# FNet mixing and an ELU layer: w_in folded with two products a chunk after sums and differences of its rows

## The chip, the core and the metric

The kernel runs on one core of one Trainium2 chip. The profile names its engines PE (TensorE, matrix products; PEld is its loading of weights), DVE (VectorE), ACT (ScalarE), POOL (GpSimd) and SP (SyncE, which here only issues DMAs). The metric is the device time of one execution in microseconds (us), the median over several.

## What is computed

```python
X = np.fft.fft(x, axis=1)          # x: (8, 3008, 256) float32
X = np.fft.fft(X, axis=2).real
t = X.reshape(24064, 256)
h = t @ w_in                       # w_in: (256, 2048), float64
g = np.where(h > 0, h, np.exp(np.minimum(h, 0)) - 1)
out = g @ w_out                    # w_out: (2048, 256), float64
```

The real part of the two transforms is cosine times cosine less sine times sine: along the sequence and along the 256 channels. The weights come as 64-bit floats, and the kernel turns them to 32 bits itself.

## The kernel before

**The channel transform is folded into w_in.** x is real, so channels d and 256-d are first added and subtracted (e and o), which leaves 129 cosine channels and 127 sine channels. The matrix of channel cosines and sines, CC, is multiplied into w_in once: Wc = cos @ w_in (128 rows) and Ws = -sin @ w_in (127 rows, and in its last row the 129th cosine channel). h is then Wc times the sequence cosines of e plus Ws times the sequence sines of o, plus the 129th channel, which lies in wex and Rb and is added on VectorE.

**Chunks of weights.** w_in and w_out are cut into eight chunks of 512 KB each. A `Chunk` is loaded (`load`, on SP) into a home `raw` and turned into 32-bit floats in steps: `fields` (L204: two TENSOR_SCALAR on VectorE, L212 and L218, take exponent and mantissa out of the high words), `power` (L224: ScalarE), `round` (L234: GpSimd adds low and high mantissa; for the very first chunk VectorE, L243) and `scale` (L249: L255 on VectorE puts sign and exponent together, then GpSimd multiplies; for the first chunk VectorE, L264). Homes are shared by chunks: those of chunks 0, 1 and 2 of w_in are used again by chunks 5, 6 and 7, and later by other tiles.

**fold_chunk (L371)** multiplies a chunk of w_in (256 rows, 256 columns; its rows lie in two halves of 128 on the partitions) by CC: two results, 128x256 for Ws and 128x256 for Wc, each as two products over 128 rows that add up in one PSUM bank, "H". `put_chunk` (L385) copies the results to Ws and Wc with two ScalarE instructions. `spread_last_row` (L390) sends the last row of Ws through DRAM into columns of wex.

**The main loop** runs over 47 tiles of 256 columns and, in each, over eight *slots*. A slot takes two of the 16 blocks of 128 rows of the hidden layer: `mm_P` (H<-Rr,Wc), `even_part` (E on VectorE, L728), `mm_Q` (H<-Ir,Ws, which adds to the same bank and so must wait until E is read), `h_minus` (L738), two ScalarE passes and two VectorE passes for the ELU (L754), and the products with w_out (pA to pD<-G). From the third tile on the products with w_out use seven products for eight, from sums of G on GpSimd and sums of w_out (`sum_weights`, WT). Tiles 0 and 1 are worked on together in the first sixteen slots and use w_out plainly; the slots of block pair i need chunk i of w_in folded and chunk i of w_out scaled.

**The sequence transform.** For each of the eight batches `fold_x` (L435) folds x: for each of four pieces j, e{j} = lo + hi, o{j} = lo - hi over channels (L441, operations e and o), a copy c{j} of channel 0 (L461), a memset z{j} of a pad column, then sums and differences between pieces (E0, EO0, O0 and so on). For the first batch all this is on VectorE, at the start; for the others on GpSimd, spread over the slots by the list FOLDS. `Dft` multiplies the folds by cosine and sine matrices MC and puts the results into rings Rr and Ir.

**The order of the work.** Each step is entered into a list of events with a due time (`at`, in slots of PERIOD = 4.8), which are made by hand; the events are sorted by due time, and compute instructions are kept in that order on each engine (`pin`). DMAs are placed by the framework. So every engine runs a fixed sequence, and waits at the first instruction whose input isn't there. Before the first product 46 products on zeros run on PE. The bank tag "H" has three buffers; fold_chunk and the slots take them in turn.

Of the kernel before, what the change touches and what calls it, by code (L numbers as in the profile page):

```python
# [9 lines left out]
FP = mybir.dt.float32  # L10
# [5 lines left out]
ALU = mybir.AluOpType  # L16
# [39 lines left out]

def _chan_consts():

    c = np.arange(256)
    d = np.arange(129)  # L60
    cos = np.cos(2.0 * np.pi * ((c[:, None] * d[None, :]) % 256) / 256)
    d = np.arange(1, 128)
    sin = -np.sin(2.0 * np.pi * ((c[:, None] * d[None, :]) % 256) / 256)
    m = np.concatenate([cos[:, :128], sin, cos[:, 128:]], axis=1)
    return np.ascontiguousarray(
        m.reshape(2, 128, 256).transpose(1, 0, 2).reshape(128, 512)
    ).astype(np.float32)


# [9 lines left out]
def kernel(  # L79
# [80 lines left out]
        return L  # L160


    CC = cpool.tile([128, 512], FP, tag="CC")
    w2 = cpool.tile([128, NF * ND], FP, tag="w2")
    Wc = cpool.tile([128, NDFF], FP, tag="Wc")
    Ws = cpool.tile([128, NDFF], FP, tag="Ws")
# [5 lines left out]
    w1 = {}  # L172

    class Chunk:

        def __init__(self, src, dst, raw, tmp, shared):
            self.src, self.dst, self.home, self.tmp_tag = src, dst, raw, tmp
            self.shared = shared  # L180

        def load(self):
            dst = self.dst()
            if not wide:
                nc.sync.dma_start(out=dst, in_=self.src)
                return
            home = self.home
            if isinstance(home, tuple):
                tag, bufs, size = home
                home = spool.tile([128, size], FP, tag=tag, bufs=bufs, name="raw")  # L190
            words = home[:, 0:1024].bitcast(I32)
            self.raw = words.rearrange("p (n w) -> p n w", w=2)
            n = dst.shape[1]
            nc.sync.dma_start(
                out=words.rearrange("p (a b) -> p a b", a=n), in_=self.src.bitcast(I32)
            )
# [37 lines left out]
        def round(self):  # L234
# [11 lines left out]
                )  # L246
            )

        def scale(self):  # L249

            if not wide:
                return
            lo, hi, dst = self.parts()
            pin(
                nc.vector.scalar_tensor_tensor(  # L255
                    out=self.t, in0=hi, scalar=-(2**31), in1=self.t,
                    op0=ALU.bitwise_and, op1=ALU.bitwise_or,
                )
            )
            if self.shared:  # L260
                gtt(dst, dst, self.t.bitcast(FP), ALU.mult)
                return
            pin(
                nc.vector.scalar_tensor_tensor(  # L264
                    out=dst, in0=dst, scalar=2.0**-20,
                    in1=self.t.bitcast(FP), op0=ALU.mult, op1=ALU.mult,
                )
            )

    def w1_dst(c):  # L270
        q, half = divmod(c, 2)
        if q not in w1:
# [24 lines left out]
            IN_HOMES[c],  # L297
            IN_TMP[c],
            c > 0,
        )  # L300
        for c in range(8)
    ]
# [4 lines left out]
            OUT_HOMES[c],  # L307
            OUT_TMP[c],
            True,
        )  # L310
        for c in range(8)
    ]
# [39 lines left out]
    def mm(out_, lhsT, rhs, start, stop=True):  # L352
        pin(
            nc.tensor.matmul(  # L354
                out_, lhsT=lhsT, rhs=rhs, start=start, stop=stop, skip_group_check=True
            )
        )
# [7 lines left out]
    def act(o, i, func=AF.Copy, **kw):  # L365
        pin(nc.scalar.activation(out=o, in_=i, func=func, **kw))  # L366
# [3 lines left out]

    def fold_chunk(c):  # L371

        q, half = divmod(c, 2)
        ps = folds[c] = bank("H")
        for n, part in enumerate((128, 0)):
            for h in range(2):
                mm(
                    ps[:, 256 * n : 256 * n + 256],
                    CC[:, h * 256 + part : h * 256 + part + 128],
                    w1[q][:, h, half * 256 : half * 256 + 256],  # L380
                    n == 0 and h == 0,
                    h == 1,
                )

    def put_chunk(c):  # L385
        cols = slice(c * 256, (c + 1) * 256)
        for n, dst in enumerate((Ws, Wc)):
            act(dst[:, cols], folds[c][:, 256 * n : 256 * n + 256])

    def spread_last_row(q):  # L390
        c = slice(q * 256, (q + 1) * 256)
# [38 lines left out]
        gtt(W[3], W[1], b21, ALU.add)  # L430


    OC = slice(0, 6 * 127)

    def fold_x(L, engine_of, pieces):  # L435

        ops = {}

        def op(key, o, a, b, f):
            tt = lambda o, a, b, f: pin(  # L440
                engine_of(key).tensor_tensor(out=o, in0=a, in1=b, op=f)  # L441
            )
            n = o.shape[1]
            cuts = [n * i // pieces for i in range(pieces + 1)]
            for i in range(pieces):
                c = slice(cuts[i], cuts[i + 1])
                ops[key, i] = lambda c=c: tt(o[:, c], a[:, c], b[:, c], f)

        E, O = [], []
        for j in range(4):  # L450
            e = spool.tile([128, 6 * 128], FP, tag=f"e{j}", bufs=1, name=f"e{j}")
            o = spool.tile([128, 6 * 127 + 1], FP, tag=f"o{j}", bufs=1, name=f"o{j}")
            ev = e.rearrange("p (m d) -> p m d", d=128)
            ov = o[:, OC].rearrange("p (m d) -> p m d", d=127)
            src = L[j].rearrange("p (m d) -> p m d", d=ND)
            if j in (1, 2):
                src = src[:, ::-1]
            lo, hi = src[:, :, 1:128], src[:, :, 255:128:-1]
            op(f"e{j}", ev[:, :, 1:128], lo, hi, ALU.add)
            ops[f"c{j}", 0] = lambda e=ev[:, :, 0:1], s=src[:, :, 0:1]: pin(  # L460
                engine_of("c").tensor_copy(out=e, in_=s)  # L461
            )
            op(f"o{j}", ov, lo, hi, ALU.subtract)
            E.append(e)
            O.append(o)
        ops["x1", 0] = lambda: act(L[1][0:1, 5 * ND :], L[0][0:1, 0:ND])
        for j in (1, 3):
            ops[f"z{j}", 0] = lambda o=O[j]: pin(
                nc.gpsimd.memset(o[:, 6 * 127 :], 0.0)
            )  # L470
        P = [o[:, OC] for o in O]
        op("E0", E[0], E[0], E[1], ALU.add)
        op("E2", E[2], E[2], E[3], ALU.add)
        op("EO0", E[1], E[0], E[2], ALU.add)
        op("EO1", E[3], E[0], E[2], ALU.subtract)
        op("O0", P[0], P[0], P[1], ALU.subtract)
        op("O2", P[2], P[2], P[3], ALU.subtract)
        op("EO2", P[1], P[0], P[2], ALU.subtract)
        op("EO3", P[3], P[0], P[2], ALU.add)
        return [E[1], E[3], O[1], O[3]], ops  # L480

    FOLDS = (
        "c0 e0 c3 e3 c2 e2 x1 c1 e1 E0 E2 EO0 o0 o3 o2 o1 z1 z3 O0 O2 EO2 EO1 EO3".split()
    )

    def fold_first(L):
# [45 lines left out]
    class Dft:  # L532
# [5 lines left out]
            self.ring = ring if ring is not None else (Ir if ri else Rr)  # L538

        def mms(self, par, ps):  # L540
            width = 1 if self.first else 127 if self.ri else 128
            dft_mms(ps, self.ri, self.kodd, par, self.stat, width)
            if par:
                self.pb = ps
            else:
                self.pa = ps
# [515 lines left out]
        state["x_even"] = Dft(0, 0, 0, fold_first(L_first), ring=Rb, first=True)  # L1062

    at(-25.5, load_rest)
    at(-25.0, lambda: fold_now("z1 z3 c3 e3"))
    at(-24.9, w1_chunks[0].scale)
    at(-24.8, lambda: fold_now("o3 c2 e2 E2 o2 O2"))
    at(-24.5, begin_x_even)
    at(-24.4, lambda: fold_now("c0 e0 c1 e1 E0 EO0"))
    at(-20.7, lambda: load_mats(1, 1))  # L1070
    at(-20.6, w1_chunks[5].load)
    at(-20.5, w2_chunks[5].load)
# [25 lines left out]
    for chunk, k in (  # L1098
        (w2_chunks[0], 0),
        (w1_chunks[2], 1),  # L1100
        (w1_chunks[3], 2),
        (w2_chunks[1], 3),
        (w1_chunks[4], 4),
        (w2_chunks[2], 5),
        (w1_chunks[5], 6),
        (w2_chunks[3], 7),
        (w1_chunks[6], 8),
        (w2_chunks[4], 9),
        (w1_chunks[7], 10),
        (w2_chunks[5], 11),  # L1110
        (w2_chunks[6], 12),
        (w2_chunks[7], 14),
    ):
        t = k * T
        first = ((0.96, 0.96, 0.97, 1.9), (3.0, 3.05, 3.06, 4.22), (0.95, 0.96, 0.97, 4.2))
        dt = first[k] if k < 3 else (-0.5, 0.05, 0.06, 2.95)
        for d, fn in zip(dt, (chunk.fields, chunk.power, chunk.round, chunk.scale)):
            at(t + d, fn)
    for chunk, t in (
# [156 lines left out]
    at(27 * T + 1.0, lambda: ext_rows(0, vtt))  # L1276
    at(27 * T + 1.46, lambda: ext_side(3))
    at(28 * T + 1.35, lambda: ext_rows(1, gtt))
    fold_keys = [(k, p) for k in FOLDS for p in range(2 if k[0] not in "czx" else 1)]
    n_big = sum(k[0] not in "czx" for k, _ in fold_keys)  # L1280
    for b in range(1, NB):
        s0 = (b - 1) * steps_b
        l0 = s0 - 8 if b > 1 else 5.2
# [4 lines left out]
        for key in fold_keys:  # L1288
            at(
                int(f0 + n * (f1 - f0) / n_big) * T + 1.3,  # L1290
                lambda key=key: state["ops"][key](),
            )
            n += key[0][0] not in "czx"
        for n, (ri, kodd) in enumerate(((0, 0), (1, 0), (0, 1), (1, 1))):
            at_dft(
                s0 + (28, 34, 38, 42)[n], 2, b, ri, kodd,
# [56 lines left out]
```

## Time and profile before

| | |
|---|---|
| median of 8 runs | 1972.76 us (1971.12 to 1979.74) |
| the profiled execution | 1971.63 us, of which the span of the profile is 1969.8 us |
| busy: PE, DVE, ACT, POOL | 1957.5, 1274.7, 869.5, 1333.0 us |
| fold products H<-w,CC | 64 records, 15.1 us busy |
| scaling and rounding of weights on POOL, 128x512 | 1.3 us each |
| one sum of G on POOL, 128x256 | 728 ns |
| a copy of a fold result on ACT, 128x256 | 378 ns |

How to read it: the span is from the first instruction to the last. A 32-bit product of PE leaves two MATMUL records in the profile, so the 32 fold products are 64 records. A record's own time overlaps the next one's, so what a product takes is read from the distance of two starts. In a row of the timeline the first number is the start in us, the second the duration, and the bracket at the end tells the idle time before it and who ended it. A row "x8" is eight instructions in a row.

### The profile page before, as it was taken

What the parts mean: (1) busy time and instruction counts of PE and PEld (TensorE: products, weight loads), DVE (VectorE), ACT (ScalarE), POOL (GpSimd) and SP (SyncE); (2) the same over time, 40 slices, a digit from 0 to 9 for tenths busy, and PEclk for the clock granted to TensorE, in tenths of its full rate; (3) what the DMA queues carried; (4) which work ended last, traced back from release to release, by engine and by line L of the source; (5) the groups of instructions that cost most, each with busy time, mean ns of one, the idle gap of its engine ahead of it and who ended that gap; (6) DMA issues with size and microseconds to landing.
All of it is one profiled execution on the core that took longest, in us unless ns stands there. A gap on an engine that the chain in (4) does not pass through costs nothing.

```text
span 1969.8 us, 26831 instructions
## 1 busy us (share of the span) xinstructions
PE 1957.5 (99%) x8900; PEld 1662.8 (84%) x8900; DVE 1274.7 (65%) x2325; ACT 869.5 (44%) x1667; POOL 1333.0 (68%) x1804
## 2 busy tenths in 40 slices
PE   9999999999999999999999999999999999999998
PEld 5888888888888888888888888888888888888887
DVE  8866656765666656666566665676566665666666
ACT  4654444444444444444344444444434444344443
POOL 3588657775677766777567875778657776455655
PEclk9999999999999999999999999999999999999999
DMA  9056200121001110021100301013010110100101
GB/s 367 22 21 91 38 11 20 47 48 22 12 20 46 45 27 11 18 65 27 26 18 13 79 12 26 11 19 91 6 20 12 20 22 15 16 12 12 22 10 24
DMA packets 255610, 71.08 MB, mean 36 GB/s; under 512 B 243998, under 2 KB 244786, under 8 KB 255088
## 3 DMA queue, kind: packets, MB, share of 16 engines
q1 hardware_dynamic: 250896, 56.52, 15.0%
q0 software_dynamic: 2400, 12.59, 1.9%
q8 instruction: 70, 1.15, 0.2%
q14 instruction: 68, 0.56, 0.1%
q10 hardware_dynamic: 2176, 0.26, 0.1%
HBM read 44.50 MB, written 24.80 MB: 35 GB/s over the span
## 4 chain that ended last, share of the span: by engine, by line
PE 95%; DVE 2%; issue 1%; POOL 1%; ACT 0%; DMA 0%; DVEq 0%; POOLq 0%
PE H L354 39%; PE pD L354 16%; PE pB L354 16%; PE pC L354 16%; PE pA L354 8%; DVE E L728 0%; DMA wex<-wx 0%; POOL xl L145 0%; POOL G L363 0%; DVE v L360 0%; DVE G L754 0%; ACT G L366 0%; ACT M L366 0%; DVE Ir L360 0%; DVE u L360 0%
## 5 line engine op out<-in xcount | busy, mean ns | idle before, releaser
L363 POOL TENSOR_TENSOR G<-G 128x256 f32<-128x256 f32 x1440 | 1034.8, 728 | 566.9 <-DVE G L754 455.3
L728 DVE SCALAR_TENSOR_TENSOR E<-Rb,wex,H 128x256 f32<-128x256 f32 x752 | 328.1, 478 | 613.5 <-PE H L354 609.7
L366 ACT ACTIVATE G<-H 128x512 f32<-128x512 f32 x376 | 224.5, 597 | 953.2 <-DVE G L738 953.1
L354 PE MATMUL H<-Ir,Ws 128*128 128x256 f32 x1504 | 387.2, 380 | 1.9 <-DVE E L728 1.8
L354 PE MATMUL H<-Rr,Wc 128*128 128x256 f32 x1504 | 386.4, 379 | 0.0
L354 PE MATMUL pC<-G,WT 128*128 128x256 f32 x1440 | 369.5, 379 | 0.0
L354 PEld LDWEIGHTS H<-Rr,Wc 128*128 128x128 f32 x1504 | 285.1, 190 | 54.1 <-issue 2.5
L354 PEld LDWEIGHTS H<-Ir,Ws 128*128 128x128 f32 x1504 | 277.0, 189 | 51.6 <-DVE E L728 5.3
L354 PEld LDWEIGHTS pC<-G,WT 128*128 128x128 f32 x1440 | 273.6, 190 | 37.2
L738 DVE SCALAR_TENSOR_TENSOR G<-E,H 128x512 f32<-128x512 f32 x376 | 257.3, 684 | 37.1 <-PE H L354 1.6
L754 DVE SCALAR_TENSOR_TENSOR G<-G,H 128x512 f32<-128x512 f32 x376 | 255.9, 680 | 25.9 <-ACT G L366 25.9
L754 DVE SCALAR_TENSOR_TENSOR G<-M,G 128x512 f32<-128x512 f32 x376 | 257.0, 684 | 0.0
L366 ACT ACTIVATE G<-G 128x512 f32<-128x512 f32 x376 | 233.2, 620 | 0.0
L354 PE MATMUL pA<-G,w 128*128 128x256 f32 x784 | 229.4, 379 | 0.2 <-POOL w L363 0.2
L354 PE MATMUL pB<-G,w 128*128 128x256 f32 x784 | 229.2, 379 | 0.0
L354 PE MATMUL pD<-G,w 128*128 128x256 f32 x784 | 229.2, 379 | 0.0
L366 ACT ACTIVATE M<-G 128x512 f32<-128x512 f32 x376 | 224.3, 596 | 0.0
L366 ACT ACTIVATE M<-M 128x512 f32<-128x512 f32 x376 | 220.9, 588 | 0.1
L354 PE MATMUL pD<-G,WT 128*128 128x256 f32 x720 | 214.4, 379 | 1.6 <-DVE v L360 1.6
L354 PE MATMUL pB<-G,WT 128*128 128x256 f32 x720 | 214.4, 379 | 0.5 <-POOL G L363 0.5
L354 PEld LDWEIGHTS pA<-G,w 128*128 128x128 f32 x784 | 148.9, 190 | 20.8 <-POOL w L363 0.6
L354 PEld LDWEIGHTS pD<-G,w 128*128 128x128 f32 x784 | 149.0, 190 | 20.2
(132 smaller groups left out, 1385.4 us busy)
## 6 DMA issues: line engine op xcount, KB each, us to landing
out_dram<-ot SPq DMA_DIRECT2D x496, 32.0 KB
xl<-in_x_dram SPq DMA_DIRECT2D x16, 768.0 KB
out_dram<-ot SPq DMA_DIRECT2D x256, 2.0 KB
Rb<-r SPq DMA_DIRECT2D x10, 376.0 KB
raw<-in_moe_w_in_dram SPq DMA_DIRECT2D x7, 512.0 KB
MC<-dft_mats SPq DMA_DIRECT2D x3, 1131.0 KB
raw<-in_moe_w_out_dram SPq DMA_DIRECT2D x5, 512.0 KB
out_dram<-ot SPq DMA_DIRECT2D x64, 28.0 KB
```

The source lines that it names most:

```text
L354: nc.tensor.matmul(out_, lhsT=lhsT, rhs=rhs, start=start, stop=stop, skip_group_check=True)
L363: pin(nc.gpsimd.tensor_tensor(out=o, in0=a, in1=b, op=op))
L366: pin(nc.scalar.activation(out=o, in_=i, func=func, **kw))
L728: nc.vector.scalar_tensor_tensor(out=S.E[:, c], in0=Rb[:, cols(i)], scalar=wex[:, f : f + 1], in1=S.H[:, c], op0=ALU.mult, op1=ALU.add,)
L738: nc.vector.scalar_tensor_tensor(out=two(S.G[:, 0:512])[:, :, ::-1], in0=two(S.E), scalar=2.0, in1=two(S.H), op0=ALU.mult, op1=ALU.subtract,)
L754: nc.vector.scalar_tensor_tensor(out=o, in0=e, scalar=-1.0, in1=h, op0=ALU.add, op1=ALU.max)
```

## The change

The 256 rows c of w_in are taken as pairs c and c+128. The cosine or sine of channel frequency d at c+128 is that at c for even d and its negative for odd d. So after scaling, GpSimd makes w[c] + w[c+128] and w[c] - w[c+128] (`pair`, two products of 128x256 into the chunk's home, `ab`), and fold_chunk needs one product over 128 rows for all even frequencies and one for all odd ones. CC has 256 columns instead of 512.

The even product holds 64 cosine rows, 63 sine rows and the 129th cosine row; the odd one 64 sine and 64 cosine rows. put_chunk therefore copies halves of 64 partitions: four a chunk instead of two, and for chunks 2 to 7 the two for Wc are on VectorE.

Wc and Ws now have their rows in the order even, odd (or odd, even), and the folds of x must come out in the same order: fold_x writes e and o as [6][2][64] and reads x with a step of two channels. All 128 columns are written at once, so the copy c comes after its e, and the pad column of o (and the memset z) is gone: that column is x[128] - x[128].

The event list differs for the first slots: the fields of chunk 2 of w_in are due earlier and those of chunk 3 of w_in later.

```diff
 def _chan_consts():
-    c = np.arange(256)
...
+    c = np.arange(128)[:, None]
+    def block(fn, d):
+        return fn(2.0 * np.pi * ((c * d[None, :]) % 256) / 256)
+    even, odd = np.arange(0, 129, 2), np.arange(1, 128, 2)
+    return np.concatenate([
+        block(np.cos, np.roll(even[:64], -1)), -block(np.sin, even[1:64]),
+        block(np.cos, even[64:]), -block(np.sin, odd), block(np.cos, odd)], axis=1)
...
+        def pair(self):
+            dst = self.dst()
+            gtt(self.ab[:, 0:256], dst[:, 0], dst[:, 1], ALU.add)
+            gtt(self.ab[:, 256:512], dst[:, 0], dst[:, 1], ALU.subtract)
         def scale(self):
+            self.multiply()
+            if self.pairs:
+                self.pair()
...
     def fold_chunk(c):
         ps = folds[c] = bank("H")
-        for n, part in enumerate((128, 0)):
-            for h in range(2):
-                mm(ps[:, 256 * n : 256 * n + 256],
-                   CC[:, h * 256 + part : h * 256 + part + 128],
-                   w1[q][:, h, half * 256 : half * 256 + 256],
-                   n == 0 and h == 0, h == 1)
+        for n in range(2):
+            cols = slice(256 * n, 256 * n + 256)
+            mm(ps[:, cols], CC[:, 128 * n : 128 * n + 128],
+               w1_chunks[c].ab[:, cols], n == 0)
     def put_chunk(c):
-        for n, dst in enumerate((Ws, Wc)):
-            act(dst[:, cols], folds[c][:, 256 * n : 256 * n + 256])
+        for dst in (Ws, Wc):
+            for half in range(2):
+                p = slice(64 * half, 64 * half + 64)
+                n = half ^ (dst is Ws)
+                src = folds[c][p, 256 * n : 256 * n + 256]
+                if dst is Ws or c < 2:
+                    act(dst[p, cols], src)
+                else:
+                    pin(nc.vector.tensor_copy(out=dst[p, cols], in_=src))
...
-            lo, hi = src[:, :, 1:128], src[:, :, 255:128:-1]
-            op(f"e{j}", ev[:, :, 1:128], lo, hi, ALU.add)
+            lo, hi = (t.rearrange("p m (d o) -> p m o d", o=2)
+                      for t in (src[:, :, 1:129], src[:, :, 255:127:-1]))
+            op(f"e{j}", ev, lo[:, :, ::-1], hi[:, :, ::-1], ALU.add)
...
-        "c0 e0 c3 e3 c2 e2 x1 c1 e1 E0 E2 EO0 o0 o3 o2 o1 z1 z3 O0 O2 EO2 EO1 EO3"
+        "e0 c0 e3 c3 e2 c2 x1 e1 c1 E0 E2 EO0 o0 o3 o2 o1 O0 O2 EO2 EO1 EO3"
...
-    at(-25.0, lambda: fold_now("z1 z3 c3 e3"))
+    at(-25.0, lambda: fold_now("e3 c3"))
-    at(-24.8, lambda: fold_now("o3 c2 e2 E2 o2 O2"))
+    at(-24.8, lambda: fold_now("o3 e2 c2 E2 o2 O2"))
-    at(-24.4, lambda: fold_now("c0 e0 c1 e1 E0 EO0"))
+    at(-24.4, lambda: fold_now("e0 c0 e1 c1 E0 EO0"))
...
-        first = ((0.96, 0.96, 0.97, 1.9), (3.0, 3.05, 3.06, 4.22), (0.95, 0.96, 0.97, 4.2))
-        dt = first[k] if k < 3 else (-0.5, 0.05, 0.06, 2.95)
+        first = ((0.96, 0.96, 0.97, 1.9), (2.1, 2.9, 2.91, 4.22),
+                 (2.95, 2.96, 2.97, 4.2), (0.95, 0.96, 0.97, 4.2))
+        dt = first[k] if k < 4 else (-0.5, 0.05, 0.06, 2.95)
```

On the engines this moves the following instructions: PE's fold products go from four to two a chunk, and the rest of its order is unchanged. VectorE's order changes at slots 1 to 4: the L212 and L218 of w_in's chunk 2 stand ahead of the ELU of slot 0, those of w_in's chunk 3 behind the ELU of slot 1, and those of w_out's chunk 1 behind E of slot 3. ScalarE works on w_in's chunk 2 ahead of the ELU of slot 1. On SP the load of w_in's chunk 2 stands ahead of that of MC[1, 0].

## Prediction

> **What bounds the kernel now.** I read the page first (shares, then the chain), then the waits of TensorE, then windows and the timeline of the first 140 us.
>
> ```profile
> PE 1957.5 (99%) x8900; PEld 1662.8 (84%) x8900; DVE 1274.7 (65%) x2325; ACT 869.5 (44%) x1667; POOL 1333.0 (68%) x1804
> ...
> PE 95%; DVE 2%; issue 1%; POOL 1%; ACT 0%; DMA 0%; DVEq 0%; POOLq 0%
> ```
>
> TensorE is busy nearly always and 95% of the chain that ends last runs through it, so a product taken away is worth its own time wherever the next product is ready. The granted clock is 0.9 or more in all 40 slices. A busy PE is no proof that PE is the limit (ends are modelled), so I checked the spacing of its records: a 128x256 product leaves two records, and eight records of one chunk stand from 65.18 to 66.91 us, 0.216 us each. That spacing holds from 102 us to the end but for a few gaps under 0.8 us. The slack lies in the first 100 us:
>
> ```profile
> 13.22 1.89 PE L354 MATMUL H<-w,CC 128*128 128x256 f32 x8
> ...
> 15.46 2.17 PE L354 MATMUL pC<-MC,xe 128*128 128x377 f32 x6 [0.35 <-DVE xe L360]
> ...
> 39.74 1.32 DVE L212 TENSOR_SCALAR pow<-raw 128x512 int32<-128x512 int32 x1
> ...
> 40.98 1.49 DVE L218 TENSOR_SCALAR w<-raw 128x512 int32<-128x512 int32 x1
> ...
> 45.84 1.49 DVE L212 TENSOR_SCALAR pow<-w 128x512 int32<-128x512 int32 x1
> 47.25 0.41 DVE L218 TENSOR_SCALAR w<-w 128x512 int32<-128x512 int32 x1
> 47.59 0.86 DVE L728 SCALAR_TENSOR_TENSOR E<-Rb,wex,H 128x256 f32<-128x256 f32 x2
> ...
> 48.51 1.13 PE L354 MATMUL H<-Ir,Ws 128*128 128x256 f32 x4 [1.45 <-DVE E L728]
> ```
>
> These are timeline rows (start, duration, engine, what, then the idle before and who ended it). Two things are to be seen. At 15.46 and 48.51 PE waits for VectorE. And L212 and L218, which take 0.42 to 0.43 us where GpSimd rests (4.17, 30.20), take 1.3 to 1.5 us where a GpSimd product runs (39.49 to 42.18): there they stand until it ends. Near 94 us GpSimd is what is late:
>
> ```profile
> 93.17 1.27 POOL L363 TENSOR_TENSOR w<-w,pow 128x512 f32<-128x512 f32 x1
> ...
> 94.50 1.99 PE L354 MATMUL pA<-G,w 128*128 128x256 f32 x8 [0.21 <-POOL w L363]
> ```
>
> PE's gaps, from distances of starts less records times 0.216: 0.51 at 15.46, 0.34 at 28.99, 0.61 at 39.88, 1.71 at 48.51, 0.28 at 88.84, 0.48 at 94.50.
>
> **What goes.** Eight chunks lose two of four products each: 4 records x 0.216 = 0.86 us a chunk, 6.9 us in all. This is the gross gain. I follow each chunk to see what is late next.
>
> Chunk 0 (13.22): PE would be free at 14.1 instead of 14.95, but its next product waits for xe from VectorE at 15.45. Its 0.86 is lost.
>
> Copies c behind sums e (VectorE, start): each e now writes column 0 too and c must follow it. Dependent rows stand 0.98 us apart (e2 at 11.18, E2 at 12.16), independent ones 0.87, and one after a small row 0.20 (xg 14.96, xd 15.16). Counting on, xe comes 0.12 later and E0 0.38 later, so the product pA, which had no more than 0.06 us to spare at 19.37, starts 0.35 later. At 28.99 PE's gap of 0.34 then falls away, since PE itself is later: -0.35 and +0.34.
>
> Chunk 1 gains 0.86. The pair (two GpSimd 128x256 products, 0.73 each by the costliest row of the page, 1.46 a chunk) follows the scaling that ends at 28.5 and is done about when PE comes, 30.0 to 30.5. But ScalarE has two more instructions (64x256 halves; partitions don't shorten a row, the 32x752 copy takes 0.83, so two halves cost one 128x256 row more each, spaced 0.27: +0.55), and VectorE gets to EO1 late: PE waits 0.26 for it.
>
> Chunks 2 and 3 gain 0.86 each. Here VectorE's order changes. The fields of chunk 2 of w_in move into 1.1 us of idle before L754 at 34.72, so its pair (42.1) meets PE's arrival (41.6 for the first product, which needs only the sums). The gap at 39.88 shrinks from 0.61 to 0.24: +0.37. E of slot 3 no longer stands behind L212/L218 of w_out's chunk 1 (1.75 us from 45.84 to 47.59), but behind two new PSUM copies of 64x256. No row shows these; from 0.17 (copy of 128x6) to 0.41 (TENSOR_TENSOR 128x256 with PSUM) each, I take 0.3, nearest to the latter's spacing. PE comes 1.7 us earlier, and the gap of 1.71 becomes 0.93: +0.78.
>
> The price: those fields now come after E, near 45.9, and PE needs w_out's chunk 1 for slot 2. From its L212 to the end of its scaling it took 45.84 to 52.49, 6.65 us, of which some 1.9 are such stands (L212 1.49, L255 1.50 against 0.43 and 0.69). From 45.9 it is ready between 50.7 and 52.5; PE arrives at 50.4. A new wait of 0.3 to 2.1; I take 1.2.
>
> [...]
>
> Chunks 4 and 5 gain 0.86 each in full: w_out's chunks 2 and 3 are scaled at 65.2 and 80.05 and used at 67.8 and 81.75, and before the E rows VectorE idles 1.3 to 2.2 us, which covers the copies.
>
> Chunk 6 loses its 0.86: the product at 94.50 waits for w_out's chunk 4, whose path (ScalarE at 89.42, GpSimd to 94.44) doesn't get shorter. The pair itself fits into the idle 0.97 us ahead of 90.11, with c0 moved behind.
>
> Chunk 7: w_out's chunk 5 is ready at 108.48 and used at 108.88. Of 0.86, 0.36 remains: -0.50. The pair fits into 2.27 us of idle before 102.26. From there GpSimd is full to 136.4 and then waits 0.82 for VectorE; it begins 3 to 4 us earlier with the rest, so the cover stays. Were it gone, each pair would cost 1.46.
>
> Hidden: memsets (16 x 0.1 us on GpSimd) go; folds of 384 for 381 columns, 1%, under GpSimd's idle 0.77 us a slot at 150 to 173; CC is 128 KB less, and w_in's chunk 2 is issued before MC[1,0] on SP, which was held at 14.65: about 1.3 us more ahead of it less 0.3 for CC, landing near 22.6 instead of 21.6, needed at 23.4. Later loads into homes that PE now frees wait some us more, tens of us before use.
>
> **Step 2 reads.** The folds now read every second element in both inputs. No row shows that for two inputs; for one, VectorE's L255 (high words) takes 0.69 like L264 (dense), and GpSimd's w<-raw,w 1.29 to 1.33 against 1.27 to 1.29. From 0 to a doubling (0.95 on VectorE, 1.0 on GpSimd) a fold; I take 0, the nearest rows.
>
> **Sum.** 6.91 - 0.86 - 0.35 + 0.34 - 0.26 + 0.37 + 0.78 - 1.2 - 0.86 - 0.50 = 4.4 us saved. The profiled execution took 1971.63 (span 1969.8 and 1.8 around it) and would take 1967.3; the median of the eight runs, 1972.76, is 1.1 higher: 1968.4.
>
> **Rivals.**
> 1. The waits are covered: PE takes nearly all, 5 to 7 us, 1966 to 1967.5. For it: 65% VectorE, gaps at 39.88 and 48.51 that the new order removes. Against: w_out's readiness at 94.50 and 108.88 leaves little.
> 2. Given back: VectorE's and GpSimd's stands grow with the pairs, the first stretch stays bound by them and 0 to 2.5 us is saved, 1970.3 to 1972.8. For it: VectorE 18.63 of 20 us busy at 40 to 60 us. Against: later stretches still give 1.7.
> 3. Slower: the step-2 reads double the folds. GpSimd has 3.03 us of sums and a 1.0 us fold in a slot of 4.75, so it decides from 1.77 us a fold; at 2.0, 0.23 us x some 96 folds is 22 us, with seven folds at 0.95 on VectorE at the start: near 1990. Against: the rows with one such input.
> That the products don't go is excluded: PE's order shows two where four stood, nothing else on PE moved.
>
> **How the numbers follow.** Forecast 1968.4, from 1967.5 to 1970.3: 0.49. Rival 1: 0.24. Rival 2: 0.16. Rival 3: 0.11. About 0.2%, 3.9 us, is what a measurement of this kernel can tell from no change (1968.8). Of the forecast about two thirds lie beyond it, 0.32, with rival 1 0.56 faster; the rest and most of rival 2 within, 0.32; slower 0.12. The range takes in rivals 1 and 2 and leaves out the third: 1965.3 to 1973.0.
>
> **What would show it.** H<-..,CC with 32 records; the gap at 15.46 near 1.5; the one at 48.51 under 1; a new wait of PE for POOL w or for G near 51; the one at 94.50 near 1.3. VectorE's and GpSimd's fold rows at 0.95 and 1.0. It is wrong if folds are longer, if PE waits for the pair, or if the gaps' sum before 100 us, now 3.9, passes 9.

## The result, and the profile after

The changed kernel takes **1979.74 us** (median of 16 runs, 1976.68 to 1982.35) against 1971.99 for the kernel before (43 runs): 1.0034 of it, 95% interval 1.0026 to 1.0041. It is slower by 7.8 us; the forecast was 1968.4. The profiled execution has a span of 1977.6 us, 7.8 more than before.

The first lines of the page of the changed kernel, in the order of those of before: busy time and share of the span with the number of records, and the shares of the chain that ended last.

```profile
PE 1956.1 (99%) x8868; PEld 1658.3 (84%) x8868; DVE 1280.2 (65%) x2337; ACT 872.1 (44%) x1671; POOL 1366.8 (69%) x1804
...
PE 95%; DVE 2%; POOL 1%; ACT 1%; issue 1%; DMA 0%; POOLq 0%; DVEq 0%
```

PE has 32 records fewer, as was to be, and its busy time is 1.4 us less, not 6.9. POOL is busy 34 us longer. POOL stands with 1% in the chain of both kernels, so the shares alone don't tell where the time went. PE's rows do. (Start, duration, engine, line, tiles; in the bracket the idle time and who ended it. L378 is the product, L754 E, L387 a GpSimd product, L468 a fold, L417 the new PSUM copy.) Timeline of the changed kernel, PE alone:

```profile
15.34 2.17 PE L378 MATMUL pC<-MC,xe 128*128 128x377 f32 x6 [1.26 <-DVE xe L384]
...
47.89 1.13 PE L378 MATMUL H<-Ir,Ws 128*128 128x256 f32 x4 [1.56 <-DVE E L754]
...
53.73 1.99 PE L378 MATMUL pA<-G,w 128*128 128x256 f32 x8 [1.26 <-POOL w L387]
...
83.79 1.13 PE L378 MATMUL H<-Ir,Ws 128*128 128x256 f32 x4 [1.12 <-DVE E L754]
...
95.75 2.41 PE L378 MATMUL pA<-G,w 128*128 128x256 f32 x8 [1.99 <-POOL w L387]
...
114.70 3.44 PE L378 MATMUL pA<-G,w 128*128 128x256 f32 x8 [3.58 <-POOL w L387]
```

By distances of starts less the records' own time, PE's gaps are 1.42 at 15.34, 0.42 at 32.03, 0.25 at 39.39, 0.34 at 43.04 (inside a fold product), 1.73 at 47.89, 1.42 at 53.73, 0.38 at 69.28, 1.28 at 83.79, 2.15 at 95.75 and 3.75 at 114.70. These sum to 9.6 ahead of 100 us, and 3.75 more. Measured in the same way those of before sum to 3.4 ahead of 100 us, with none of that size behind. (The prediction's 3.9 counts 0.10 us more at five of its six gaps: the first record behind such a gap stands 0.32 us from the next, not 0.216.) The last two rows show a second thing: eight records take 2.41 and 3.44 us where a run of eight takes 1.89. Soon after those two waits records stand 0.427 us apart instead of 0.216. The stretches of the changed kernel around them, PE alone (window, its length, PE busy and records, granted clock, DMA):

```profile
93.77:97.18 3.41, 1.43 (x7) 1.00 0.04 1
97.18:100.60 3.42, 3.42 (x10) 0.50 0.00 0
100.60:104.01 3.41, 3.41 (x20) 1.00 0.26 65
110.84:114.25 3.41, 0.28 (x2) 1.00 0.04 1
114.25:117.66 3.41, 2.96 (x7) 0.50 0.00 0
117.66:121.08 3.42, 3.42 (x17) 1.00 0.00 0
```

The granted clock is one half for 3.41 us, twice. The first of these stretches has 10 records where 20 would go. In the kernel before it is 1.00 everywhere between the start and the last microseconds. The two halved stretches cost some 1.7 and 1.55 us (the second is less, since PE still waits at its start), the waits ahead of them 2.15 and 3.75. Compared product by product, PE is 0.3 us behind the kernel before at the product at 89.17, 1.3 behind at the product at 95.75, 2.9 behind at 101.95, and 7.4 behind at 117.98; from there to the end 0.4 is added.

Who made PE wait at 114.70 is read from GpSimd's rows in the changed kernel:

```profile
104.53 1.29 POOL L387 TENSOR_TENSOR w<-raw,w 128x512 f32<-128x512 f32 x1 [2.50 <-ACT w L390]
110.33 0.46 POOL L387 TENSOR_TENSOR WT<-w 128x128 f32<-128x128 f32 x1 [4.51 <-PE H L378]
...
112.09 0.20 POOL L493 COPY e<-xl 128x6 f32<-128x6 f32 x1
112.24 1.18 POOL L468 TENSOR_TENSOR e<-xl 128x384 f32<-128x384 f32 x1
113.37 1.27 POOL L387 TENSOR_TENSOR w<-w,pow 128x512 f32<-128x512 f32 x1
```

and from those of the kernel before, where the same sum follows without a wait:

```profile
103.52 0.45 POOL L363 TENSOR_TENSOR WT<-w 128x128 f32<-128x128 f32 x1
...
107.22 1.26 POOL L363 TENSOR_TENSOR w<-w,pow 128x512 f32<-128x512 f32 x1
```

In the changed kernel GpSimd is idle for 4.51 us, until PE is done with a product into H. The waiting instruction is the first of sum_weights: it writes WT, and WT2 lies in the home that w_in's chunk 7 had. Before, PE read that chunk from w1 and the home was long free; now PE reads the sums and differences (`ab`) from the home, so WT can't be written until PE has folded chunk 7 (109.22). Queued behind on GpSimd are three more sums, a copy, a fold, and then the scaling of w_out's chunk 5 (113.37), for which PE's very next products wait. Without the 4.51 us, by these rows, that scaling would have ended at 110.13 instead of 114.64, ahead of PE at 110.95.

### The profile page after: what moved, and what is told of

It is laid out like the page before. It is cut to its first block, busy times and chain, and to the rows that moved or that the text cites. A ratio compares the mean times of both kernels' runs of the same rounds, so it can differ in the third digit from the quotient of the medians.

```text
span 1977.6 us, 26798 instructions
## 1 busy us (share of the span) xinstructions
PE 1956.1 (99%) x8868; PEld 1658.3 (84%) x8868; DVE 1280.2 (65%) x2337; ACT 872.1 (44%) x1671; POOL 1366.8 (69%) x1804
## 4 chain that ended last, share of the span: by engine, by line
PE 95%; DVE 2%; POOL 1%; ACT 1%; issue 1%; DMA 0%; POOLq 0%; DVEq 0%
PE H L378 38%; PE pB L378 16%; PE pD L378 16%; PE pC L378 16%; PE pA L378 8%; POOL w L387 1%; DMA xl<-in_x_dram,ix 0%; DVE E L754 0%; DVE e L468 0%; DVE G L780 0%; ACT G L390 0%; POOL G L387 0%; POOL e L468 0%; ACT M L390 0%; DVE v L384 0%
## 5 line engine op out<-in xcount | busy, mean ns | idle before, releaser
L387 POOL TENSOR_TENSOR G<-G 128x256 f32<-128x256 f32 x1440 | 1037.1, 730 | 546.5 <-DVE G L780 436.0
L754 DVE SCALAR_TENSOR_TENSOR E<-Rb,wex,H 128x256 f32<-128x256 f32 x752 | 328.0, 477 | 604.9 <-PE H L378 601.8
L378 PE MATMUL H<-Ir,Ws 128*128 128x256 f32 x1504 | 388.5, 381 | 3.0 <-DVE E L754 2.9
L378 PE MATMUL H<-Rr,Wc 128*128 128x256 f32 x1504 | 386.4, 379 | 0.0
L378 PE MATMUL pC<-G,WT 128*128 128x256 f32 x1440 | 369.5, 379 | 0.0
L378 PEld LDWEIGHTS H<-Rr,Wc 128*128 128x128 f32 x1504 | 285.1, 190 | 54.1 <-issue 2.5
L378 PEld LDWEIGHTS H<-Ir,Ws 128*128 128x128 f32 x1504 | 277.9, 189 | 53.3 <-DVE E L754 7.8
L378 PEld LDWEIGHTS pC<-G,WT 128*128 128x128 f32 x1440 | 273.6, 190 | 37.2
L378 PE MATMUL pA<-G,w 128*128 128x256 f32 x784 | 231.4, 382 | 6.8 <-POOL w L387 6.8
L378 PE MATMUL pB<-G,w 128*128 128x256 f32 x784 | 229.7, 380 | 0.0
L378 PE MATMUL pD<-G,w 128*128 128x256 f32 x784 | 229.3, 379 | 0.0
L378 PE MATMUL pD<-G,WT 128*128 128x256 f32 x720 | 214.4, 379 | 1.6 <-DVE v L384 1.6
L378 PE MATMUL pB<-G,WT 128*128 128x256 f32 x720 | 214.6, 380 | 0.6 <-POOL G L387 0.6
L378 PEld LDWEIGHTS pA<-G,w 128*128 128x128 f32 x784 | 149.9, 192 | 28.5 <-POOL w L387 8.0
L378 PEld LDWEIGHTS pB<-G,w 128*128 128x128 f32 x784 | 149.4, 191 | 20.5
```

Of the source, the lines that this page charges most:

```text
L378: nc.tensor.matmul(out_, lhsT=lhsT, rhs=rhs, start=start, stop=stop, skip_group_check=True)
L387: pin(nc.gpsimd.tensor_tensor(out=o, in0=a, in1=b, op=op))
L754: nc.vector.scalar_tensor_tensor(out=S.E[:, c], in0=Rb[:, cols(i)], scalar=wex[:, f : f + 1], in1=S.H[:, c], op0=ALU.mult, op1=ALU.add,)
```

## The experiments

| run | median us | against before | 95% interval |
|---|---|---|---|
| the change | 1979.74 | 1.0034 | 1.0026 to 1.0041 |
| e1: first sums of w_out later | 1975.40 | 1.0021 | 1.0010 to 1.0032 |
| e2: folds read with unit step | 1976.97 | 1.0027 | 1.0016 to 1.0037 |
| e4: no sums and differences | 1977.96 | 1.0028 | 1.0014 to 1.0042 |
| e5: VectorE's copies first | 1978.91 | 1.0034 | 1.0021 to 1.0047 |
| e7: step of two in the last sums | 1976.94 | 1.0027 | 1.0015 to 1.0039 |
| e8: four edits | 1969.69 | 0.9985 | 0.9975 to 0.9996 |
| e9: six edits | 1968.37 | 0.9977 | 0.9967 to 0.9987 |
| e10: e9 and earlier fields | 1971.29 | 0.9990 | 0.9979 to 1.0001 |
| e11: old order of the first slots | 1985.06 | 1.0057 | 1.0041 to 1.0072 |
| b1: edits of e9 on the kernel before | 1971.01 | 1.0000 | 0.9988 to 1.0011 |
| p1, p2: filler on GpSimd in the kernel before | 1977.21, 1977.78 | 1.0024, 1.0028 | 1.0007 to 1.0040, 1.0015 to 1.0042 |

The theory: two waits of PE for GpSimd and the halved clock behind each make the loss, one from the home of chunk 7, the other from longer folds and the pair ahead of w_out's chunk 4. The rival: GpSimd's 34 us of added work, over the whole run.

**e1, the home.**

```diff
-        at((11 + 0.7 * i) * T + 1.0, lambda i=i: sum_weights(i))
+        at((11 + 0.7 * i) * T + (1.0 if i else 2.96), lambda i=i: sum_weights(i))
```

> The changed kernel, with the first step of sum_weights (the one that writes WT into the home of w_in's chunk 7) moved behind the scaling of w_out's chunk 5. My theory: PE's wait of 3.75 us for POOL w at 114.70 is POOL's own wait of 4.51 us for PE's fold of chunk 7, since WT is written over the words that this fold now reads; and PE's records 0.427 us apart for some 3 us after it are a lower clock that follows the wait. Then POOL's wait goes, PE's wait near 114 falls under 0.8 us, the records after it stand 0.216 apart, and 4.5 to 5.5 us are saved: 1974.2 to 1975.2 instead of 1979.7. Rival: POOL is late there by the sum of its pairs and longer folds, and the wait for PE only fills time that is lost anyway: the gap stays over 2.3 us and less than 2 us is saved.

Measured 1975.40, 4.3 us less than the change: a little under the range, far from the rival. PE's rows of this kernel:

```profile
110.44 1.03 PE L378 MATMUL H<-Rr,Wc 128*128 128x256 f32 x4
111.30 1.89 PE L378 MATMUL pA<-G,w 128*128 128x256 f32 x8
113.68 1.13 PE L378 MATMUL H<-Ir,Ws 128*128 128x256 f32 x4 [0.49 <-DVE E L754]
```

The product pA now follows without a wait and its eight records take 1.89 again; 0.65 us for E is late next. GpSimd still waits for PE ahead of WT, but only 0.85 us, and chunk 5 is scaled by then. The wait at 96.10 and its halved clock are still there. So the wait for the home is shown to cost some 4.3 us.

**e2 and e7, the step of two.** e2 takes the step out, e7 puts it elsewhere with the right result.

```diff
 e2
-                t.rearrange("p m (d o) -> p m o d", o=2)
+                t.rearrange("p m (o d) -> p m o d", o=2)
 e7
-            op(f"e{j}", ev, lo[:, :, ::-1], hi[:, :, ::-1], ALU.add)
+            op(f"e{j}", ev, lo, hi, ALU.add)      # one channel after another
...
-        op("EO0", E[1], E[0], E[2], ALU.add)
+        op("EO0", blocks(E[1]), steps(E[0], 1), steps(E[2], 1), ALU.add)
```

> The changed kernel, but the folds of x read their channels one after another instead of with a step of two; the channels then come in an order that doesn't fit the rows of Wc and Ws, so the result is another one than the reference's, with the same instructions and sizes. Theory: the step costs GpSimd 0.18 us a fold (1.19 against 1.0) and VectorE nothing. Then e and o on GpSimd fall from 1.19 to 1.0 us, the rounding and scaling of w_out's chunk 4 end 0.4 to 0.8 us earlier, PE's wait of 2.15 at 95.75 falls to 1.4 to 1.8 us, and if that is short enough for the records after it to stand 0.216 apart, 1.7 us more is saved: 0.5 to 2.5 us in all, 1977.2 to 1979.2. Rival A: the step is what made the kernel slower (96 folds): 4 us or more is saved. Rival B: the 1.19 comes from contention with VectorE and not from the step: the fold rows stay at 1.19 and nothing is saved.

> The changed kernel, with the even-odd order made in the last four sums of a fold (EO0 to EO3) and not in the eight first ones: e and o read one channel after another again, only EO0 to EO3 read with a step of two. The result is the reference's. Theory: the step costs GpSimd 0.18 us an instruction wherever it stands, so e and o on GpSimd return to 1.0 us, EO0 to EO3 rise to 1.2, and the first 100 us go as in the kernel with unit steps: PE's wait near 95.7 is 1.8 us or less, the records after it stay 0.216 apart, about 2.5 us saved, 1976.5 to 1978. The wait near 113 for the home stays above 3 us. Rival: the gain of the unit-step run came from something else in it (its values, or luck of the clock): no gain, 1979 or more.

The folds on GpSimd, grouped by line and shape (count, busy us, mean ns, idle before), in the changed kernel:

```profile
L468 POOL TENSOR_TENSOR e<-xl 128x384 f32<-128x384 f32 x56 | 67.1, 1199 | 0.0
L468 POOL TENSOR_TENSOR o<-xl 128x384 f32<-128x384 f32 x56 | 66.2, 1181 | 0.0
L468 POOL TENSOR_TENSOR e<-e,e 128x384 f32<-128x384 f32 x56 | 56.0, 1001 | 0.6
```

in e2:

```profile
L468 POOL TENSOR_TENSOR e<-xl 128x384 f32<-128x384 f32 x56 | 56.7, 1014 | 0.0
```

and in e7:

```profile
L468 POOL TENSOR_TENSOR e<-e,e 128x384 f32<-128x384 f32 x56 | 60.9, 1089 | 0.6
L468 POOL TENSOR_TENSOR e<-xl 128x384 f32<-128x384 f32 x56 | 57.0, 1018 | 0.0
```

In e7 half of the 56 rows e<-e,e read with the step: a mean of 1.09 is 1.0 for the one half and 1.18 for the other. So 0.18 us goes with the step wherever it stands. On VectorE the steps cost nothing: o<-xl took 0.95 us with and without. Both kernels take 1977.0, 2.8 us less than the change, a little more than I expected of e2 and within the range for e7. Of the 2.8 only 0.3 and 0.2 are shorter waits of PE (1.81 and 1.84 instead of 2.15, and 3.55 and 3.57 instead of 3.75); 1.7 is the clock, which stayed full behind the first of them. In e7:

```profile
97.00:100.60 3.60, 3.60 (x19) 1.00 0.01 2
113.33:116.75 3.42, 3.42 (x10) 0.50 0.00 0
```

A step that adds 0.18 us an instruction cost 2.8 us, because it lengthened one wait from some 1.8 us, behind which the granted clock stayed 1.00, to 2.15 us, behind which it was 0.50 for 3.41 us. In the later slots it costs nothing that shows: e7 has 56 longer folds there and e2 none, and they take the same time.

**e4, the pair.**

```diff
-            if self.pairs:
+            if self.pairs and False:
                 self.pair()
```

> The changed kernel without the sums and differences on GpSimd: the fold products read the raw words of the home instead, so the result is another one, and all waits for the home stay as they are. Theory: of PE's waits, those at 42 to 43 (0.5 us together) and most of 95.75 (2.15 us, of which 1.95 is the pair of chunk 6 ahead of w_out's chunk 4) are GpSimd's time for the pairs, and that at 114.70 is not (WT still has to wait for PE's fold of chunk 7): 2 to 4.5 us saved, the wait near 114 stays over 3 us: 1975.2 to 1977.7. Rival: the pairs' time on GpSimd is the whole loss: both waits go, and 6 us or more is saved, 1973.5 or less.

1977.96: 1.8 less by the medians, a little under the range, and the interval doesn't tell it from the change. The wait at 43.04 goes, the one for E near 47.5 grows from 1.73 to 2.36, and the one before w_out's chunk 4 falls from 2.15 to 1.41 and keeps the full clock. Product by product, PE is then 3.1 us ahead of the changed kernel. The wait for the home stays (3.73 at 111.57), but is followed by two halved stretches instead of one, which takes 1.4 us back. The pairs are part of the loss, not the whole: the rival's 1973.5 is refuted.

**e5, the copies.**

```diff
-        for dst in (Ws, Wc):
+        for dst in (Ws, Wc) if c < 2 else (Wc, Ws):
```

> The changed kernel, with the order of the four PSUM copies of chunks 2 to 7 changed: VectorE's two for Wc are entered ahead of ScalarE's two for Ws, so that VectorE doesn't wait for ScalarE. Theory: PE's waits for E at 47.89 (1.73), 69.28 (0.38) and 83.79 (1.28) come from VectorE waiting up to 6.7 us at its copies for ScalarE's, which stand behind ELU passes. Then the waits at 69.28 and 83.79 go and the one at 47.89 falls under 1.2, but PE then comes earlier to the waits for w_out's chunks 1, 4 and 5, which take back what lies ahead of them: 0 to 1 us is saved in all, 1978.7 to 1979.7, with the wait at 95.75 up to 1.7 us longer. Rival A: those waits are real losses to the end, 1.5 to 2.5 us saved. Rival B: ScalarE's copies, now behind VectorE's, come later, and PE's products with Ws wait for them instead: 0 to 2 us slower.

1978.91. PE's waits at 69.28 and 83.79 are gone and the one at 47.89 is 1.12; that at 95.75 is 2.53, and the one for the home 4.19 with two halved stretches. The time is in the theory's range, but not for its reason. Compared product by product with the changed kernel, e5 is 2.0 us ahead before the wait for w_out's chunk 4, which takes back only 0.4; the clock then stays full, and e5 is 3.3 ahead at 102 us. The longer wait for the home and its second halved stretch leave 1.7 at 130 us, and a late transfer near 184 us (see e11) takes 1.1 more. VectorE's rows in the changed kernel:

```profile
43.51 2.05 DVE L468 TENSOR_TENSOR o<-o,o 128x768 f32<-128x768 f32 x1
46.09 0.86 DVE L417 COPY Wc<-H 64x256 f32<-64x256 f32 x2 [0.53 <-ACT Ws L390]
46.96 0.87 DVE L754 SCALAR_TENSOR_TENSOR E<-Rb,wex,H 128x256 f32<-128x256 f32 x2
```

and in e5:

```profile
45.47 0.85 DVE L417 COPY Wc<-H 64x256 f32<-64x256 f32 x2
46.35 0.87 DVE L754 SCALAR_TENSOR_TENSOR E<-Rb,wex,H 128x256 f32<-128x256 f32 x2
```

In the changed kernel VectorE waits for ScalarE's copies of the same bank before it can start its own, and E, for which PE waits, is queued behind. In the list of waits of the changed kernel that stand is 6.7 us in five places, 2.2 the longest.

**e11, the order of the first slots** (the due times of w_in's chunks 2 and 3 and w_out's chunk 1 as before the change).

> The changed kernel with the due times of the first slots as they were before the change: the fields of w_in's chunk 2 late in slot 1 again, those of chunk 3 early in slot 2, E of slot 3 behind the fields of w_out's chunk 1. My prediction gave the new order +0.37 and +0.78 us and took 1.2 for a new wait for w_out's chunk 1: nearly nothing in all. Theory: the wait near 53.7 goes, that near 48 grows to 2.2 to 3.5 us (E behind fields and copies), and the time is within 1 us of the changed kernel's 1979.7. Rival A: the new order was itself a loss: 1 us or more faster. Rival B: without it the pair of chunk 2 is late: 1 us or more slower.

1985.06, 5.3 us slower than the change: Rival B's side, for another reason than the pair. PE's rows of e11:

```profile
41.20 1.13 PE L378 MATMUL H<-Ir,Ws 128*128 128x256 f32 x4 [1.60 <-DVE E L754]
...
51.73 1.97 PE L378 MATMUL H<-Ir,Ws 128*128 128x256 f32 x4 [3.31 <-DVE E L754]
```

The wait near 53.7 is gone, but E comes 1.76 and 3.48 us late, and behind the longer wait four records take 1.97 us, where a run of four takes 1.13 behind the other. Product by product, e11 is 2.4 us behind the changed kernel at 130 us. Most of the rest is a wait of 3.0 us at 189.90, which the changed kernel's profile doesn't have: PE waits for xe, and GpSimd, which makes it, waits for the transfer xs<-xe_dr of the 129th channel, issued at 185.60 where the changed kernel issues it at 170.85. Such a wait of 1.0 to 1.7 us is in the profiles of e5, e8 and p2 too, and p2 has nothing of the change; why the transfer is late is open. So by the trace the new order was worth 2.4 us and was no part of the loss; whether the other 2.9 belong to the order isn't shown.

**p1 and p2, a wait alone.** The kernel before, nothing of the change, with two and five sums of zeros on GpSimd ahead of the scaling of w_out's chunk 4.

```diff
+    for _ in range(5):
+        at(9 * T + 2.94, lambda: gtt(fill, fill, fill, ALU.add))
```

> The kernel before, with two sums of 128x256 of zeros on GpSimd (0.73 us each by the trace) put in ahead of the scaling of w_out's chunk 4; nothing of the change is in it. PE's wait at 94.50 should grow from 0.4 to about 1.9 us. Theory (a wait of PE over some 2 us is followed by a halved clock, one under 1.8 is not): on the border; if the clock stays full, 1.5 us are lost, 1973.5, if not 3.2, 1975.2. Rival (the halved clock belongs to the changed kernel): 1.5 us are lost.

> The same with five such sums, 3.65 us. PE's wait at 94.50 grows to about 4 us. Theory: the granted clock then is one half for some 3.4 us or twice that behind the wait, and the loss is 3.65 and 1.5 to 3 more: 5.2 to 6.7 us, 1977.2 to 1978.7. Rival: the clock stays full in the kernel before, 3.65 us lost, 1975.7.

p2: a wait of 4.14 us at 98.59, one halved stretch behind it, and 5.7 us lost (1977.78 against 1972.04), within the theory's range and over the rival's 3.65. PE alone in p2:

```profile
96.34:99.75 3.41, 1.16 (x5) 1.00 0.04 0
99.75:103.17 3.42, 3.42 (x9) 0.50 0.00 0
103.17:106.58 3.41, 3.41 (x20) 1.00 0.00 0
```

The halved clock belongs to the wait, not to the change. p1's profile has a wait of 1.64 us and a full clock; its ten runs lie in two groups, 1972.9 to 1976.0 at a mean clock of 0.999 and 1978.4 to 1984.4 at 0.998 or less. The median of 1977.21 fits neither 1973.5 nor 1975.2. Three of the lower runs (1972.9 to 1973.3) are what a wait of 1.5 us costs, but one halved stretch is 1.7 us and the upper group is 2.4 to 11.5 above the lower one. The profile shows a run of the lower kind, so what fills the rest is open.

**e8, e9 and e10, the change repaired.** e8 has the edits of e1, e5 and e7, and the second batch's folds begin at slot 10. e9 also puts those folds and the third step of sum_weights behind the scalings of their slots. e10 moves the fields of w_out's chunk 1 too.

```diff
 e8 (with those of e1, e5 and e7)
-        f0, f1 = (s0 - 1, s0 + 38) if b > 1 else (8, 37)
+        f0, f1 = (s0 - 1, s0 + 38) if b > 1 else (10, 37)
 e9
-                int(f0 + n * (f1 - f0) / n_big) * T + 1.3,
+                k * T + (3.0 if k < 16 else 1.3),      # k as before
-        at((11 + 0.7 * i) * T + (1.0 if i else 2.96), lambda i=i: sum_weights(i))
+        at((11 + 0.7 * i) * T + (2.96 if i == 0 else 1.1 if i == 2 else 1.0), ...)
 e10
-            (0.95, 0.96, 0.97, 4.2),
+            (0.02, 0.96, 0.97, 4.2),
```

> Four edits on the changed kernel together: WT's first sums behind the scaling of w_out's chunk 5, VectorE's copies ahead of ScalarE's, the step of two in EO0 to EO3 only, and the folds of the second batch begun at slot 10 instead of 8, so that none stands ahead of w_out's chunk 4 on GpSimd. If the waits near 95.7 and 114 and the halved clock behind them are what the change lost, all of them go: from 1979.7 by 4.3 (WT), 2.8 (step) and some 2 more (waits for E at 69 and 84, folds ahead of chunk 4), 1969 to 1971.5, faster than the kernel before (1972.0). Rival: something the change does all through the run (later slots) costs too; then it stays above 1972.5.

> The kernel with the four edits, and two more: in slots 10 to 15 each fold of the second batch stands behind the scaling due in that slot instead of ahead of it, and the third step of sum_weights behind the scaling of w_out's chunk 6. They are aimed at PE's waits of 0.79 us at 105.95 (a copy and a fold ahead of chunk 5's scaling, 1.4 us) and 1.0 us at 117.42 (sums of w_out ahead of chunk 6's). Theory: both waits go and 1 to 1.8 us are saved, 1968 to 1968.8. Rival: PE, come earlier, waits for the same data a slot later; under 0.5 us saved.

> As the last, and VectorE's two fields of w_out's chunk 1 are entered at the start of slot 3, ahead of the PSUM copies and E. In the changed kernel PE waits 1.73 us at 47.89 for E and 1.42 at 53.73 for w_out's chunk 1; with the copies swapped, 1.12 and 1.35. Theory: w_out's chunk 1 is what sets the end of this stretch, so with the fields 1.6 us earlier the second wait falls by 1 us or more, the first grows by 0.8 or less, and 0.3 to 1 us is saved against the last. Rival: ScalarE's conversions of that chunk come behind its copies of Ws anyway; the first wait grows and the second stays, up to 0.8 slower.

e8: 1969.69, e9: 1968.37, both as the theory had them, and both ahead of either kernel. (The profiled run of e8, 1971.65, has the late transfer: 1.67 us of waiting at 176.89.) In e9 PE's rows where the change lost its time are without a wait:

```profile
91.41 1.89 PE L378 MATMUL pA<-G,w 128*128 128x256 f32 x8
...
105.03 1.89 PE L378 MATMUL pA<-G,w 128*128 128x256 f32 x8
```

What is left of the change's price in e9 are the waits of the first 55 us: 1.39 at 15.52, 0.42 at 32.22, 0.34 at 43.23, 1.12 at 47.48, 1.36 at 53.26.

e10 is 2.9 slower than e9, which neither the theory nor its rival had. The wait for w_out's chunk 1 is gone, but E is now 3.39 us late instead of 1.12, so that the two waits together grow from 2.48 to 3.39, and behind the one long wait the clock is halved, which costs 1.7 us; behind e9's two waits of 1.12 and 1.36 it wasn't (the mean clock of the profiled executions is 0.998 in e10 and 1.000 in e9).

**b1, the same edits without the change.**

> The kernel before, without the change, with those of the edits that can be made in it: folds of the second batch from slot 10 on and behind the scalings, and the first and third step of sum_weights behind the scalings. It tells how much of the gain of the repaired kernel is the change's own. Theory: before had only two waits of PE at these places, 0.37 us at 94.50 and none at 109, so it gains 0.2 to 0.5 us: 1971.5 to 1971.8, and the repaired kernel with the change stays 1.5 to 3 us ahead. Rival: the gain is that of the edits, and this one comes to 1970 or less.

1971.01, 0.7 to 1.0 less than the kernel before by the medians; the interval takes in no difference. The change with its repairs is 2.6 us ahead of this one, and their intervals against the kernel before (0.9967 to 0.9987, and 0.9988 to 1.0011) don't overlap. Product by product the two profiles end 2.65 us apart. So the change, repaired, is worth some 2.6 of its 6.9 us here.

## Why the prediction was wrong

The gross gain was right: 32 records at 0.216. What follows it, in the order of the sum:

- **Chunk 0**, -0.86: the gap at 15.34 is 1.42 (0.51 before). Right.
- **Copies c**, -0.35 and +0.34: 0.22 at 19.46, and the gap at 28.99 is gone. Right. **EO1**, -0.26: 0.42 at 32.03. About right.
- **Chunks 2 and 3.** The gap at 39.88 shrank to 0.25 (0.24 predicted), and the new wait for w_out's chunk 1 is 1.42 (1.2 predicted). But PE waits for the pair of chunk 2, 0.34 and 0.2 us, which the sum left out: two products took 1.83 us where VectorE worked beside them, not 1.46. And the gap at 48.51 did not fall to 0.93: it is 1.73, where the kernel before has 1.61 by the same measure. The copies take 0.42 us each, not 0.3, and I had VectorE's wait for ScalarE's copies of the same bank (0.53) not at all. EO3 took 2.05 us at 43.51, beside a rounding on GpSimd (1.30 us from 43.44); before, at 44.98, it took 0.94. The sum had no term for that.
- **Chunks 4 and 5**, full: 0.38 at 69.28 and 1.28 at 83.79 for E. "before the E rows VectorE idles 1.3 to 2.2 us, which covers the copies": the copies can't use that idle time, since ScalarE, whose two copies come first, stands behind ELU passes. e5 shows it: with the order turned both waits go.
- **Chunk 6**, -0.86, "The pair itself fits into the idle 0.97 us ahead of 90.11": it took 1.95 us there, and the two folds ahead took 2.96 instead of 2.14. The step that I took at 0 is 0.4 of that: without it, in e2 and e7, they take 2.58 and 2.60. w_out's chunk 4 was scaled 1.25 us later than before, PE's wait was 2.15 and not 1.3, and the halved clock made it 1.7 worse. e2, e4 and e7 show that step and pair each lengthen the wait. GpSimd's rows before:

```profile
85.58 2.14 POOL L441 TENSOR_TENSOR e<-xl 128x381 f32<-128x381 f32 x2
```

and after:

```profile
85.09 2.96 POOL L468 TENSOR_TENSOR e<-xl 128x384 f32<-128x384 f32 x2
...
89.56 1.95 POOL L387 TENSOR_TENSOR raw<-w 128x256 f32<-128x256 f32 x2
...
94.43 1.26 POOL L387 TENSOR_TENSOR w<-w,pow 128x512 f32<-128x512 f32 x1
```

- **Chunk 7**, -0.50: **this is the step that failed most.** It costs 5.3 us (3.75 of waiting, 1.55 of halved clock), and e1 gives 4.3 of it back with one due time. I had written that "Later loads into homes that PE now frees wait some us more, tens of us before use". I looked for DMAs into these homes and passed over WT, which is not loaded but computed into one, on GpSimd, with PE's next weights queued behind (113.37).

By these rows the sum is 6.9 gross, less 0.9 (chunk 0), 0.6 (19.46 and 32.03), 0.5 (the pair of chunk 2), 0.1 (47.89), 1.6 (53.73, and 0.2 at 55.67) and 1.7 (69.28 and 83.79), with 0.7 of old gaps that are gone, and less 0.9 in steps of 0.05 to 0.2 us, most of them the first record behind a new wait, which stands 0.32 us from the next. That leaves 1.3 us saved, all eight chunks counted, when PE comes to the wait for w_out's chunk 4. Then go 1.8 and 1.7 at chunk 6, 3.75 and 1.55 at chunk 7, and 0.4 behind 118 us: 7.9 us lost, against 7.8 measured.

My third rival ended on the right side for the wrong reason: folds a little longer (0.18, not 1.0), and not deciding in the later slots but at one place. (It counts some 96 folds with the step on GpSimd; the profile has 112.) All three signs of failure that the prediction named came true: longer folds, a wait for the pair, and gaps ahead of 100 us above 9. What no term held is the clock: 3.2 us of the 7.8.

## What to carry to other kernels

When an operand is moved to another place, list everything that is written there next, computed tiles as well as loads, and what is queued behind each: here WT gained a wait of 4.51 us for the new reader, and the scaling that stood behind it on GpSimd came late by as much. Before adding work to an engine, look at each place where another engine waits for it last, and not at its share of busy time: 69% busy, it was late at two places. And a wait of PE is to be priced with what follows it: here 1.7 us of halved clock behind the wait of 2.15 us and 1.55 behind that of 3.75, and none behind e9's two waits of 1.1 and 1.4.

## What the runs showed of the hardware

**Behind PE's waits of 2.15 us (95.75) and 3.75 us (114.70) in the changed kernel the granted clock was 0.50 for 3.41 us.** It changes in these traces only at multiples of 3.41 us from its first full state (97.18, 100.60, 114.25, 117.66 in the changed kernel). I cut the first 200 us of the 14 profiles into such windows and added up PE's idle time in each, by distances of starts. Of the windows at full clock, 12 have 2.08 us or more of it, and 11 of these are followed by a halved window; none of those with 1.97 us or less is. The exception has 2.12, so my estimate from these counts is an edge near 2.1, about 60% of a window. By the busy time that the rows of windows print, which counts a record to its modelled end, there is no exception: the 11 have 1.98 us or more without work, every other window at full clock 1.80 or less. The window ahead of a halved one was not idle: row 93.77 above has 1.43 us of busy PE in 3.41. A wait of 1.81 to 1.84 us (e2, e7) stayed free, one of 2.15 did not. One of 2.15 in e11 and one of 2.53 in e5 stayed free as well: there the windows cut the wait, and hold 1.97 and 2.12 at most. The first full state begins 4.1 to 6.0 us behind the start of the span in the 14 profiles (5.35 before, 5.03 in the changed kernel), so the windows don't lie alike over the instructions of all of them. The same kernel may then fall on either side. That fits the 16 runs of the changed kernel, which go from 1976.68 at a mean clock of 0.999 to 1982.35 at 0.997, but with one profile of each kernel it isn't shown.

**In these folds the step of two made GpSimd's rows longer, not VectorE's**: 1.18 to 1.20 us in the changed kernel against 1.0 in e2 for 128x384 sums with two stepped inputs of 32-bit words; on VectorE o<-xl, 128x768, took 0.95 in both.
